# Opening of an FFT-mix and MoE kernel: x loaded in 96 rows, stage A stored with r outermost and in an order of its own, ten buffers for it, weights begun within stage A

## The chip, the cores and the metric

The kernel runs on one core of one Trainium2 chip, as one program. The metric is the device time of an execution in microseconds (us); it is compared by the median of several runs. A core has TensorE (PE in the profile; its weight loads are PEld), VectorE (DVE), ScalarE (ACT), GpSimd (POOL) and SyncE (SP). In this kernel every DMA is issued from SP, which handles its instructions in order, and the bytes are moved by the core's 16 DMA engines.

## What is computed

x has 8 images of 3008 rows and 256 columns. Each is transformed along its rows, mixed with a complex 256x256 matrix, biased, soft-thresholded and transformed back; the 24064 resulting rows then go through two matrix products with a squared ReLU between them.

```python
X = np.fft.rfft(x, axis=1)
Yr = Xr @ w_r - Xi @ w_i + b_r
Yi = Xr @ w_i + Xi @ w_r + b_i
Yr = np.sign(Yr) * np.maximum(np.abs(Yr) - lam, 0.0)      # lam = 0.01, the same for Yi
y = np.fft.irfft(Yr + 1j * Yi, n=3008, axis=1)
h = np.maximum(y.reshape(-1, 256) @ w_in, 0.0)            # w_in 256 x 2048
out = h * h @ w_out                                       # w_out 2048 x 256
```

x is float32; the two MoE weights are float64.

## The kernel before, in words

3008 is 47 x 64, so the transform is done in two stages of small matrix products: stage A transforms over the 47 (index n1), for 24 values of r, and stage B over the 64 (index n2). Between the two the data turns round through scratch memory in DRAM: `scr1[b]` holds [24 r][64 n2][512], where the 512 are the real and imaginary part (c) times 256 columns (d). `load_b` reads it back as rows (n, c) for two values of r, a "pair"; 12 pairs make an image. Stage B is `points_b` (matmuls with the table `tB`, line 237), then the mix with the weights (`psm`), the threshold, a turn (`zh`), and the way back over the 64 (`psc`, line 522), whose result goes to a second scratch `scr2[b]` (`store_c`, line 225). Stage D reads this (`load_d`, tile `din`), transforms back over the 47 (`psd`, line 275) and splits the result into a high and a low part, `xt`, on which the MoE works.

After the opening, one long planned sequence of 416 rounds runs the MoE: `mm1` (tile `ph`) and `mm2` (tile `po`), three matmuls for each product on high and low parts, and in between, at places named in a plan, the stages A, B and D of later images. The first round needs `xt` of the first chunk, the weights `wi_` and, two rounds later, `wo_`.

The opening is the function `start` (lines 290 to 592). Its instructions are issued in the order in which they are written, each engine in its own order. It prepares image 0 fully, image 1 up to the end of its stage A, and all weights and tables.

- **Loads.** `loads` issues the table `tU`, image 0 of x in two tiles `x0` (seven transfers), the mixing weights `raw`, and the biases. x lies in memory as 94 rows: row 2*n1 + w holds 32 blocks of 256 numbers. The 94 rows become 94 partitions.
- **Stage A of image 0** (`stage_a(0)`, lines 460 to 473 and 544 to 550): 16 steps. Each multiplies 94 rows of x by `tU` into 96 rows (line 467; order of the 96: w, part, r), copies the result from PSUM to an `ev` buffer on ACT (even steps) or DVE (odd steps), and stores the two halves of 256 columns with two DMAs (line 472) whose destination has the four (n, c) rows outermost and the 24 r inside. There are three `ev` buffers. In step 9 the mixing weights are split (`tables_start`); in steps 11 and 13 `weights()` is called.
- **`weights()`** (line 446) advances every weight block under way by one step and begins the next. There are 16 blocks of 512 KB: eight of `w_in`, eight of `w_out`. The steps of a block: load; nothing; absolute value on ACT; four instructions on DVE that put together a float32 from the two words of a float64; then for `w_in` a copy on ACT and a subtraction on POOL, for `w_out` two copies on ACT and four operations on POOL, a step later the copy into `wo` on ACT, a step later the subtraction on POOL. The load buffers (`w64`) are four, of which `raw` holds two at first.
- **The pair loop** (lines 558 to 580), n = 0 to 14: iteration n issues the load of pair n + 3 (tile `bin`, four buffers) and two loads of image 1 (`x1`, in tiles that later hold `wo`), then the threshold of pair n - 2, stage B of pair n, the mix of pair n - 1, the way back and the store of pair n - 3 (tile `evc`, from the same three `ev` buffers), one step of stage A of image 1 (from n = 2), the turn of pair n - 2, and `weights()`. At n = 10 `late` issues the loads of further tables, at n = 13 it works on them.
- **The tail** (lines 581 to 592): the inverse of the first chunk (`inverse`, two loads `din`, each followed by its matmuls, copies and split), mixed with the last steps of stage A of image 1 and of `weights()`.

A DMA store or load that writes or reads a buffer holds it until it has landed; a copy that wants the buffer waits for that on its engine, and what is queued behind it on that engine waits too.

Of the kernel before, what the change touches and what calls it, by code (L numbers as in the profile page):

```python
# [34 lines left out]
P = 128  # L35
S = 3008
N1 = 47
N2 = 64
NR = 24
NPAIR = NR // 2  # L40
D = 256
# [3 lines left out]
W = 5  # L45
GROUPS = [(g, min(W, N2 - g)) for g in range(0, N2, W)]


def _f32(bits):
    return float(np.array([bits], np.uint32).view(np.float32)[0])  # L50
# [30 lines left out]
def plain_rows():  # L81

    n2 = np.arange(N2).reshape(-1, 2)
    return ((64 * np.arange(N1)[:, None, None] + 47 * n2.T[None]) % S).reshape(2 * N1, N2 // 2)


def _cs(num, den):

    num = np.asarray(num) % den
    ang = 2.0 * np.pi * num / den  # L90
    c, s = np.cos(ang), np.sin(ang)
    c = np.where((4 * num) % (2 * den) == den, 0.0, c)
    s = np.where((2 * num) % den == 0, 0.0, s)
    return c, s


def tables():

    r = np.arange(NR)
    c47, s47 = _cs(np.outer(r, r), N1)  # L100
    wt = np.full(NR, 2.0 / S)
    wt[0] = 1.0 / S
    ta = np.zeros((120, 4, 120))
    td = np.zeros((120, 4, 120))
    for k, w in enumerate((W, N2 % W)):
        eye = np.eye(w)
        n = NR * w
        for part, m in enumerate((c47, -s47)):
# [24 lines left out]
    sgn = np.ones((P, 2, NR), np.float32)  # L133
    sgn[64:, 0] = sig.T
    sgn[:64, 1] = sig.T
    sgn[64:, 1] = sig.T

    n1 = np.arange(N1)
    tu = np.zeros((N1, 2, 2, 2, NR))
    for part, m in enumerate(_cs(np.outer(n1, r), N1)):  # L140
        for w in range(2):
            tu[:, w, w, part] = -m if part else m
    tu = tu.reshape(2 * N1, 4 * NR)
    return dict(t_u=tu.astype(np.float32), t_a=ta.astype(np.float32), t_b=tb.astype(np.float32), t_m=tm.astype(np.float32),
                t_d=td.astype(np.float32), sgn=sgn)


# [10 lines left out]

@with_exitstack
def fft_mix_moe(ctx: ExitStack, tc: tile.TileContext, xp, xu, w_r, w_i, b_r, b_i,  # L160
                w_in, w_out, t_u, t_a, t_b, t_m, t_d, sgn, outT):
    nc = tc.nc
    B = xp.shape[0] + xu.shape[0]
    NPLAIN = xu.shape[0]
# [16 lines left out]
    tB = ctile("tB", [P, NR + 1, N2])  # L181
# [22 lines left out]
    scr1, scr2 = {}, {}  # L204
# [50 lines left out]
    chunks = [flat[i:i + 2] for i in range(0, len(flat), 2)]  # L255
# [34 lines left out]
    def start():  # L290

        with ExitStack() as own:
# [4 lines left out]
            def tl(tag, shape=(P, 512), dt=F32, bufs=1, name=None):  # L297
                return sb.tile(list(shape), dt, tag=tag, name=name or tag, bufs=bufs)
# [2 lines left out]
                return pp.tile([P, 512], F32, tag="f", name=name)  # L301

            tM = tl("tM", (P, P))
            tU = tl("tU", (2 * N1, 4 * NR))
            row = tl("t", name="row")[:1]
            rows = [tl(f"row{k}", (1, 2 * D), F32R) for k in range(2)]
            ones = tl("z", name="ones")[:1, :P]
            one = tMs[:1, 0, :]
            nq = N2 // 4

            x0 = [const.tile([P, nq, D], F32, tag=f"wi{k}", name=f"x0{k}") for k in range(2)]
            x1 = []

            def load_x0(k, parts):
                for g0, g1 in parts:
                    nc.sync.dma_start(out=x0[k][:2 * N1, g0:g1, :], in_=xu[0, :, nq * k + g0:nq * k + g1, :])

            def load_x1():
                i = len(x1)
                if i < nq:  # L320
                    x1.append(const.tile([P, 2, D], F32, tag=f"wo{i % 2}{i // 2}", name=f"x1{i}"))
                    nc.sync.dma_start(out=x1[i][:2 * N1], in_=xu[1, :, 2 * i:2 * i + 2, :])


            raw = [tl("w64", (P, 512, 2), bufs=4, name="raw").rearrange("p n w -> p (n w)")[:, :3 * D]
# [15 lines left out]

            def more_loads():
                dma = nc.sync.dma_start
                dma(out=tB[:, 5:], in_=t_b[:, 5:])
                dma(out=sg, in_=sgn)
                dma(out=tM, in_=t_m)

# [98 lines left out]
            def weights(begin=True):  # L446

                for p in list(going):
                    if next(p, going) is going:
                        going.remove(p)  # L450
                p = next(pending, None) if begin else None
                if p is not None:
                    next(p)
                    going.append(p)
                return bool(going)
# [4 lines left out]
            def stage_a(b):  # L460

                scratch1(b)
                v = scr1[b].rearrange("r n (c d) -> (n c) r d", c=2)
                for i in range(nq):
                    t = x1[i][:2 * N1] if b else x0[i // 8][:2 * N1, 2 * (i % 8):2 * (i % 8) + 2, :]
                    o = pst("psa")[:4 * NR]
                    nc.tensor.matmul(o, tU, t.rearrange("p k d -> p (k d)"), start=True, stop=True)
                    e = tl("ev", bufs=3, name="eva")[:4 * NR]
                    copy(i, e, o)
                    for k in range(2):  # L470
                        q = 8 * i + 4 * k
                        nc.sync.dma_start(out=v[q:q + 4], in_=e[:, k * D:k * D + D])
                    yield

            xs, pm, zs, pc, got = {}, {}, {}, {}, {}
# [51 lines left out]
                store_c(0, i, ev)  # L527

            def inverse(c, xt):
                for u in range(len(chunks[c])):  # L530
                    t = tl("xl", bufs=2, name="din")
                    load_d(c, u, t)
                    yield
                    ps = points_d(c, u, t, pst("psd"))
                    v = tl("t", name="dv")[:, :2 * NR * W].rearrange("p (k m) -> p k m", k=2)
                    xf = tl("z", name="dx")[:, :2 * N1 * W].rearrange("p (k m) -> p k m", k=2)
                    m, (hi, lo) = part_x(c, u, xt)
                    nc.scalar.copy(v[:, :, :ps.shape[3]], ps[:, :, 1])
                    unfold(c, u, ps, v, xf)
                    split(xf[:, :, :m], hi, lo)  # L540

            loads()
            a0, a1 = stage_a(0), stage_a(1)
            for i, _ in enumerate(a0):
                if i == 3:
                    nc.sync.dma_start(out=tB[:, :5], in_=t_b[:, :5])
                if i == 9:
                    tables_start()
                if i in (11, 13):
                    weights()  # L550
            for i in range(3):
                load_pair(i)
# [5 lines left out]
            for n in range(NPAIR + 3):  # L558
                load_pair(n + 3)
                load_x1()  # L560
                load_x1()
                if 0 <= n - 2 < NPAIR:
                    pair_z(n - 2)
                if n < NPAIR:
                    pair_b(n)
                if 0 <= n - 1 < NPAIR:
                    pair_mix(n - 1)
                if n >= 3:
                    pair_c(n - 3)
                    pair_out(n - 3)  # L570
                if n >= 2:
                    next(a1)
                if 0 <= n - 2 < NPAIR:
                    pair_turn(n - 2)
                if n == NPAIR - 2:
                    nc.sync.dma_start(out=tD, in_=t_d)
                    next(late)
                if n == NPAIR + 1:
                    next(late, None)
                weights()  # L580
            inv = inverse(0, xt)
            next(inv)
            next(a1, None)
            weights()
            for _ in inv:
                next(a1, None)
                weights()
            for _ in a1:
                weights()
            while weights():  # L590
                pass
            return xt
# [278 lines left out]
    with tc.manual_schedule():  # L871
        for r in range(last + LAG):
            c, j = divmod(r, NU)
            run(r, "load")
            k = r - 1
            if k in hid:
                m, _ = halves(cols[k // NU])
# [15 lines left out]
            k = r - LAG  # L893
# [10 lines left out]
    assert not plan, sorted(plan)  # L904


_INS = ["xp", "xu", "w_r", "w_i", "b_r", "b_i", "moe_w_in", "moe_w_out", "t_u", "t_a", "t_b", "t_m", "t_d", "sgn"]


# [32 lines left out]
```

## Time and profile before

| | us |
|---|---|
| median of 3 runs | 2825.17 (2823.32 to 2825.36) |
| the profiled execution | 2825.74 |
| its span, first to last instruction | 2823.9 |
| PE busy in the span | 2652.5 (94%) |
| DVE busy | 2145.0 (76%) |
| ACT busy | 2031.8 (72%) |
| POOL busy | 52.6 (2%), all before 285 us |
| first `psb` matmul (stage B of pair 0) starts | 103.76 |
| last `psc` matmul (way back of pair 11) starts | 236.83 |
| first `ph` matmul (MoE) starts | 268.18 |

How to read the rows below. In the slices, the span is cut in 40 and each digit is the busy share in tenths. A row of windows has the stretch, its length, the busy time of each engine with the number of instructions, the clock that TensorE was granted (1 is full speed), the busy share of the 16 DMA engines, and what they moved in GB/s. A row of the timeline has the start, the time, engine, line, operation, output and inputs, their shapes, how many instructions are merged, and in brackets the idle time of that engine just before and what ended it. A row of waits has who waited for whom, the total, the number of waits and the longest. `SPq` rows are DMA issues; their sizes are those of one transfer.

### The profile page before, as it was taken

To read this page: it belongs to the slowest core of one execution; us is meant where nothing else is said; L and a number is where in the kernel's file an instruction comes from. 1 tells how busy PE (TensorE), PEld (TensorE's weight loads), DVE (VectorE), ACT (ScalarE), POOL (GpSimd) and SP (SyncE) were. 2 spreads that over 40 slices of the span, in tenths; PEclk is the share of its full clock that TensorE was granted. 3 is DMA by queue.
4 is the path that set the end of the run, shared out by engine and by line. 5 is a ranking of instruction groups with operands and counts; after the bars stand their busy time and mean duration, and the time that the engine had idled before them with its cause. 6 is when DMAs were issued, how large, how long until landed. Compare 5 with 4: busy or idle time off the path is not lost.

```text
span 2823.9 us, 45012 instructions
## 1 busy us (share of the span) xinstructions
PE 2652.5 (94%) x17816; PEld 2434.8 (86%) x17816; DVE 2145.0 (76%) x3301; ACT 2031.8 (72%) x2885; POOL 52.6 (2%) x60
## 2 busy tenths in 40 slices
PE   3556999999999999999999999999999999999998
PEld 0333999899998999999998999999999999999998
DVE  0336788878887888878888888888888888777776
ACT  0234787778777778777887787877878787766665
POOL 0015000000000000000000000000000000000000
PEclk9967999999999999999999999999999999999999
DMA  1443111221113111221113111221113111000000
GB/s 61 137 135 109 40 41 51 80 69 44 48 51 95 43 59 38 79 81 43 51 40 105 50 46 46 71 86 43 51 44 98 54 44 51 30 24 23 23 25 18
DMA packets 130756, 164.37 MB, mean 58 GB/s; under 512 B 10766, under 2 KB 94464, under 8 KB 130358
## 3 DMA queue, kind: packets, MB, share of 16 engines
q1 hardware_dynamic: 130546, 161.49, 18.9%
q8 instruction: 142, 2.33, 0.3%
q14 instruction: 68, 0.56, 0.1%
HBM read 86.47 MB, written 74.97 MB: 57 GB/s over the span
## 4 chain that ended last, share of the span: by engine, by line
PE 44%; DVE 23%; ACT 18%; issue 5%; DMA 1%; ACTq 0%; DVEq 0%; SPq 0%
ACT gh L879 9%; DVE gl L887 6%; PE ph L200 6%; PE ph L201 6%; PE ph L202 6%; PE po L202 6%; PE po L201 6%; PE po L200 5%; DVE g L836 4%; ACT g L830 3%; ACT g L829 3%; DVE g L837 3%; DVE g L838 2%; PE psm L202 2%; PE psb L237 2%
## 5 line engine op out<-in xcount | busy, mean ns | idle before, releaser
L887 DVE TENSOR_TENSOR gl<-g,gh 128x1652 fp32r<-128x1652 f32 (+1 forms) x416 | 770.2, 1851 | 346.0 <-ACT gh L879 346.0
L879 ACT CAST gh<-g 128x1652 fp32r<-128x1652 f32 (+1 forms) x416 | 645.8, 1552 | 401.8 <-DVE g L838 319.5
L200 PE MATMUL po<-gh,wo 128*128 128x236 f32 (+1 forms) x2912 | 810.0, 278 | 5.1 <-DVE o L861 1.7
L201 PE MATMUL po<-gl,wo 128*128 128x236 f32 (+1 forms) x2912 | 800.0, 275 | 2.4 <-DVE gl L887 2.4
L202 PE MATMUL po<-gh,wo 128*128 128x236 f32 (+1 forms) x2912 | 800.6, 275 | 0.0
L200 PE MATMUL ph<-xt,wi 128*128 128x470 f32 (+1 forms) x1664 | 634.8, 381 | 11.9 <-ACT g L829 8.1
L201 PE MATMUL ph<-xt,wi 128*128 128x470 f32 (+1 forms) x1664 | 624.1, 375 | 4.0 <-DVE xt L783 3.9
L202 PE MATMUL ph<-xt,wi 128*128 128x470 f32 (+1 forms) x1664 | 619.0, 372 | 0.0
L200 PEld LDWEIGHTS po<-gh,wo 128*128 128x128 f32 x2912 | 556.1, 191 | 19.0 <-DVE o L861 5.9
L201 PEld LDWEIGHTS po<-gl,wo 128*128 128x128 f32 x2912 | 555.5, 191 | 8.9 <-DVE gl L887 2.8
L202 PEld LDWEIGHTS po<-gh,wo 128*128 128x128 f32 x2912 | 557.2, 191 | 0.0
L829 ACT ACTIVATE g<-ph 128x472 f32<-128x472 f32 (+1 forms) x832 | 417.6, 555 | 68.9 <-PE ph L202 68.8
L830 ACT ACTIVATE g<-g 128x944 f32<-128x944 f32 (+1 forms) x416 | 408.8, 983 | 13.2
L200 PEld LDWEIGHTS ph<-xt,wi 128*128 128x128 f32 x1664 | 315.6, 190 | 49.0 <-ACT g L829 12.6
L202 PEld LDWEIGHTS ph<-xt,wi 128*128 128x128 f32 x1664 | 314.3, 189 | 39.5
L201 PEld LDWEIGHTS ph<-xt,wi 128*128 128x128 f32 x1664 | 316.7, 190 | 34.5 <-DVE xt L783 6.9
L836 DVE TENSOR_TENSOR g<-g 128x472 f32<-128x472 f32 (+1 forms) x416 | 266.1, 640 | 38.4 <-ACT g L830 26.7
L838 DVE TENSOR_TENSOR g<-g 128x236 f32<-128x236 f32 (+1 forms) x416 | 166.5, 400 | 14.4
L837 DVE TENSOR_TENSOR g<-g 128x236 f32<-128x236 f32 (+1 forms) x416 | 166.5, 400 | 14.2
L202 PE MATMUL psm<-wm,xl 128*128 128x256 f32 (+1 forms) x552 | 162.1, 294 | 3.6 <-DVE xl L692 3.6
L200 PE MATMUL psm<-wm,xh 128*128 128x256 f32 (+1 forms) x552 | 161.4, 292 | 0.0
L201 PE MATMUL psm<-wm,xh 128*128 128x256 f32 (+1 forms) x552 | 159.6, 289 | 0.0
(107 smaller groups left out, 2804.4 us busy)
## 6 DMA issues: line engine op xcount, KB each, us to landing
bin<-s SPq DMA_DIRECT2D x96, 256.0 KB
s<-evc SPq DMA_DIRECT2D x96, 256.0 KB
din<-s SPq DMA_DIRECT2D x96, 240.0 KB
xin<-in_xp_dram SPq DMA_DIRECT2D x72, 240.0 KB
s<-eva SPq DMA_DIRECT2D x72, 240.0 KB
outT_dram<-o SPq DMA_DIRECT2D x96, 118.0 KB
outT_dram<-o SPq DMA_DIRECT2D x96, 117.0 KB
s<-eva SPq DMA_DIRECT2D x64, 96.0 KB
```

The source lines that it names most:

```text
L200: nc.tensor.matmul(out, l0, r0, start=start, stop=False, **kw)
L201: nc.tensor.matmul(out, l0, r1, start=False, stop=False, **kw)
L202: nc.tensor.matmul(out, l1, r0, start=False, stop=stop, **kw)
L237: nc.tensor.matmul(ps[:, k, :, q, :], tv[:, q, k], tB[:, 0:r + 2:r + 1], start=True, stop=True)
L829: nc.scalar.activation(g[:, t:4:2, :m], ph[:, :, t * t0:t * t0 + m], AF.Relu)
L830: nc.scalar.activation(g[:, 0:4, :m], g[:, 0:4, :m], AF.Square)
L836: nc.vector.tensor_sub(g[:, 4:6, :m], g[:, 1:4:2, :m], g[:, 0:2, :m])
L837: nc.vector.tensor_sub(g[:, 6, :m], g[:, 3, :m], g[:, 4, :m])
L838: nc.vector.tensor_sub(g[:, 1, :m], g[:, 6, :m], g[:, 2, :m])
L879: nc.scalar.copy(gg[k][0][:, :, :m], hid[k][:, :, :m])
L887: nc.vector.tensor_sub(gg[k][1][:, :, :m], hid.pop(k)[:, :, :m], gg[k][0][:, :, :m].bitcast(F32))
```

## The change

It is all in the opening and in its tables.

- x of images 0 and 1 is laid out in 96 rows: the last two repeat the first two, and `tU` has zeros for them. The tiles are loaded and multiplied with 96 partitions.
- The columns of `tU` are reordered, so that stage A's 96 result rows stand in the order r, w, part.
- Image 1's stage A stores have r outermost in memory and the four (n, c) rows inside; where each number ends up is unchanged.
- Image 0's stage A result is stored with one DMA a step, all 512 columns of a row in one piece. The rows of `scr1[0]` then stand in another order than those of `scr1[1]`. A reordered table `t_b0` makes up for it while image 0 is worked on; after that the whole of `tB` is loaded again from `t_b`.
- Image 0's stage A results use buffers of three tags in turn, four of `bin`, three of `ev`, three of `ld`: ten.
- `weights()` is called in steps 9, 11, 13 and 15 of stage A, and in the pair loop only up to n = 12.
- `late` issues its loads at n = 7 in place of 10.
- The step of stage A of image 1 at n = 14 is left out of the loop. After the loop both `din` loads are issued, then the load of `tB`, then the four steps of stage A that remain, with `weights()` after the second and the fourth, then the inverse, then the rest of `weights()`.

```diff
+NU1 = 96
...
     rows = ((64 * np.arange(N1)[:, None, None] + 47 * n2.T[None]) % S).reshape(2 * N1, N2 // 2)
+    return np.concatenate([rows, rows[:NU1 - 2 * N1]])
...
-    tu = np.zeros((N1, 2, 2, 2, NR))
+    tu = np.zeros((NU1 // 2, 2, NR, 2, 2))
     for part, m in enumerate(_cs(np.outer(n1, r), N1)):
         for w in range(2):
-            tu[:, w, w, part] = -m if part else m
-    tu = tu.reshape(2 * N1, 4 * NR)
+            tu[:N1, w, :, w, part] = -m if part else m
+    tu = tu.reshape(NU1, 4 * NR)
+
+    tb0 = tb.reshape(N2 // 4, 2, 2, 2, NR + 1, N2).transpose(0, 2, 3, 1, 4, 5).reshape(P, NR + 1, N2)
...
-                    nc.sync.dma_start(out=x0[k][:2 * N1, g0:g1, :], in_=xu[0, :, nq * k + g0:nq * k + g1, :])
+                    nc.sync.dma_start(out=x0[k][:NU1, g0:g1, :], in_=xu[0, :, nq * k + g0:nq * k + g1, :])
...
-                    nc.sync.dma_start(out=x1[i][:2 * N1], in_=xu[1, :, 2 * i:2 * i + 2, :])
+                    nc.sync.dma_start(out=x1[i][:NU1], in_=xu[1, :, 2 * i:2 * i + 2, :])
...
-                dma(out=tB[:, 5:], in_=t_b[:, 5:])
+                dma(out=tB[:, 5:], in_=t_b0[:, 5:])
...
-                v = scr1[b].rearrange("r n (c d) -> (n c) r d", c=2)
+                v = scr1[b].rearrange("r n (c d) -> r (n c) d", c=2)
...
-                    e = tl("ev", bufs=3, name="eva")[:4 * NR]
+                    tag, n = ("ev", 3) if b else (("bin", 4), ("ev", 3), ("bin", 4), ("ld", 3))[i % 4]
+                    e = tl(tag, bufs=n, name="eva")[:4 * NR]
                     copy(i, e, o)
-                    for k in range(2):
+                    if b == 0:
+                        v0 = scr1[b].rearrange("r n e -> r (n e)")[:, 4 * i * 2 * D:4 * (i + 1) * 2 * D]
+                        nc.sync.dma_start(out=v0.rearrange("r (m e) -> r m e", m=4), in_=e)
+                    for k in range(2 * b):
                         q = 8 * i + 4 * k
-                        nc.sync.dma_start(out=v[q:q + 4], in_=e[:, k * D:k * D + D])
+                        nc.sync.dma_start(out=v[:, q:q + 4], in_=e[:, k * D:k * D + D])
...
-                for u in range(len(chunks[c])):
-                    t = tl("xl", bufs=2, name="din")
+                got = [tl("xl", bufs=2, name="din") for _ in chunks[c]]
+                for u, t in enumerate(got):
                     load_d(c, u, t)
-                    yield
+                yield
+                for u, t in enumerate(got):
                     ps = points_d(c, u, t, pst("psd"))
...
                 if i == 3:
-                    nc.sync.dma_start(out=tB[:, :5], in_=t_b[:, :5])
+                    nc.sync.dma_start(out=tB[:, :5], in_=t_b0[:, :5])
                 if i == 9:
                     tables_start()
-                if i in (11, 13):
+                if i in (9,11,13,15):
                     weights()
...
-                if n >= 2:
+                if 2 <= n < NPAIR + 2:
                     next(a1)
...
-                if n == NPAIR - 2:
+                if n == NPAIR - 5:
                     nc.sync.dma_start(out=tD, in_=t_d)
                     next(late)
                 if n == NPAIR + 1:
                     next(late, None)
-                weights()
+                if n < NPAIR + 1:
+                    weights()
             inv = inverse(0, xt)
             next(inv)
-            next(a1, None)
-            weights()
+            nc.sync.dma_start(out=tB, in_=t_b)
+            for i, _ in enumerate(a1):
+                if i % 2 == 1:
+                    weights()
             for _ in inv:
-                next(a1, None)
-                weights()
-            for _ in a1:
-                weights()
+                pass
             while weights():
                 pass
```

More of the change, by code (lines that the diff above doesn't have):

```diff
@@ L83, in plain_rows @@
     n2 = np.arange(N2).reshape(-1, 2)
-    return ((64 * np.arange(N1)[:, None, None] + 47 * n2.T[None]) % S).reshape(2 * N1, N2 // 2)
+    rows = ((64 * np.arange(N1)[:, None, None] + 47 * n2.T[None]) % S).reshape(2 * N1, N2 // 2)
+    return np.concatenate([rows, rows[:NU1 - 2 * N1]])
 def _cs(num, den):
@@ L138, in tables @@
     n1 = np.arange(N1)
-    tu = np.zeros((N1, 2, 2, 2, NR))
+    tu = np.zeros((NU1 // 2, 2, NR, 2, 2))
     for part, m in enumerate(_cs(np.outer(n1, r), N1)):
         for w in range(2):
-            tu[:, w, w, part] = -m if part else m
-    tu = tu.reshape(2 * N1, 4 * NR)
-    return dict(t_u=tu.astype(np.float32), t_a=ta.astype(np.float32), t_b=tb.astype(np.float32), t_m=tm.astype(np.float32),
+            tu[:N1, w, :, w, part] = -m if part else m
+    tu = tu.reshape(NU1, 4 * NR)
+    tb0 = tb.reshape(N2 // 4, 2, 2, 2, NR + 1, N2).transpose(0, 2, 3, 1, 4, 5).reshape(P, NR + 1, N2)
+    return dict(t_u=tu.astype(np.float32), t_a=ta.astype(np.float32), t_b=tb.astype(np.float32), t_b0=tb0.astype(np.float32), t_m=tm.astype(np.float32),
                 t_d=td.astype(np.float32), sgn=sgn)
@@ L160, in fft_mix_moe @@
 def fft_mix_moe(ctx: ExitStack, tc: tile.TileContext, xp, xu, w_r, w_i, b_r, b_i,
-                w_in, w_out, t_u, t_a, t_b, t_m, t_d, sgn, outT):
+                w_in, w_out, t_u, t_a, t_b, t_b0, t_m, t_d, sgn, outT):
     nc = tc.nc
@@ L303, in start @@
             tM = tl("tM", (P, P))
-            tU = tl("tU", (2 * N1, 4 * NR))
+            tU = tl("tU", (NU1, 4 * NR))
             row = tl("t", name="row")[:1]
@@ L462, in stage_a @@
                 scratch1(b)
-                v = scr1[b].rearrange("r n (c d) -> (n c) r d", c=2)
+                v = scr1[b].rearrange("r n (c d) -> r (n c) d", c=2)
                 for i in range(nq):
-                    t = x1[i][:2 * N1] if b else x0[i // 8][:2 * N1, 2 * (i % 8):2 * (i % 8) + 2, :]
+                    t = x1[i][:NU1] if b else x0[i // 8][:NU1, 2 * (i % 8):2 * (i % 8) + 2, :]
                     o = pst("psa")[:4 * NR]
                     nc.tensor.matmul(o, tU, t.rearrange("p k d -> p (k d)"), start=True, stop=True)
-                    e = tl("ev", bufs=3, name="eva")[:4 * NR]
+                    tag, n = ("ev", 3) if b else (("bin", 4), ("ev", 3), ("bin", 4), ("ld", 3))[i % 4]
+                    e = tl(tag, bufs=n, name="eva")[:4 * NR]
                     copy(i, e, o)
-                    for k in range(2):
+                    if b == 0:
+                        v0 = scr1[b].rearrange("r n e -> r (n e)")[:, 4 * i * 2 * D:4 * (i + 1) * 2 * D]
+                        nc.sync.dma_start(out=v0.rearrange("r (m e) -> r m e", m=4), in_=e)
+                    for k in range(2 * b):
                         q = 8 * i + 4 * k
-                        nc.sync.dma_start(out=v[q:q + 4], in_=e[:, k * D:k * D + D])
+                        nc.sync.dma_start(out=v[:, q:q + 4], in_=e[:, k * D:k * D + D])
                     yield
@@ L904, in fft_mix_moe @@
     assert not plan, sorted(plan)
-_INS = ["xp", "xu", "w_r", "w_i", "b_r", "b_i", "moe_w_in", "moe_w_out", "t_u", "t_a", "t_b", "t_m", "t_d", "sgn"]
+_INS = ["xp", "xu", "w_r", "w_i", "b_r", "b_i", "moe_w_in", "moe_w_out", "t_u", "t_a", "t_b", "t_b0", "t_m", "t_d", "sgn"]
 def kernel(**inputs):
```

## The prediction

> **What bounds the kernel now.** I read the page first: its slices, to see where TensorE is not full.
>
> ```profile
> span 2823.9 us, 45012 instructions
> ...
> PE   3556999999999999999999999999999999999998
> ...
> DMA  1443111221113111221113111221113111000000
> ```
>
> A slice is 70.6 us. Only the first four are short of TensorE work; from the fifth on PE is full. The profiled execution took 2825.74 us, 1.84 more than its span, and the median of the runs shown is 2825.17, 0.57 below it. Next come the stretches of the opening (columns: stretch, length, busy PE, PEld, DVE, ACT, POOL, granted clock, DMA share of 16 engines, GB/s).
>
> ```profile
> 0.00:103.70 103.70, 30.60 (x32) 7.17 (x32) 8.03 (x13) 9.70 (x16) 0.20 (x4) 1.00 0.23 82
> 103.70:131.00 27.30, 27.24 (x108) 19.81 (x109) 16.33 (x27) 11.22 (x20) 3.94 (x3) 1.00 0.48 157
> 131.00:241.00 110.00, 70.11 (x210) 40.92 (x209) 49.74 (x89) 40.32 (x78) 21.62 (x27) 0.75 0.46 146
> 241.00:268.20 27.20, 8.57 (x23) 4.34 (x21) 16.73 (x18) 12.10 (x24) 25.63 (x27) 0.56 0.16 50
> 268.20:284.00 15.80, 12.26 (x42) 10.02 (x43) 5.34 (x8) 7.45 (x9) 1.18 (x1) 0.76 0.20 62
> 284.00:2640.00 2356.00, 2330.29 (x16269) 2193.05 (x16268) 1920.85 (x2966) 1832.37 (x2594) 0.00 (x0) 1.00 0.19 55
> ```
>
> After 284 us TensorE is busy 2330 of 2356 us, and the change touches nothing there. So the question is how much earlier the first `ph` matmul (268.18 us) can start. Up to 241 us no engine is full, and the DMA engines seem idle by half. Fine windows (length, PE, clock, DMA share, GB/s) show otherwise:
>
> ```profile
> 2.00:4.00 2.00, 0.00 (x0) 1.00 0.11 30
> ...
> 36.00:38.00 2.00, 2.00 (x3) 1.00 0.13 53
> ...
> 82.00:84.00 2.00, 0.00 (x0) 1.00 0.27 96
> ...
> 106.00:108.00 2.00, 2.00 (x9) 1.00 1.03 373
> ...
> 140.00:142.00 2.00, 0.00 (x0) 0.50 0.13 51
> ```
> ```profile
> 254.00:254.50 0.50, 0.00 (x0) 0.50 0.68 258
> ```
>
> While only x loads of 94 rows run, the share stands at 0.13, which is 2 of 16 engines (0.125), each at some 25 GB/s. While only stage A stores run, whose outermost dimension counts 4, it is 0.27, 4 of 16, at 24 GB/s each. Loads of 128 rows fill all sixteen. The `din` load, with 24 outermost in memory and 120 partitions, reaches 0.68, 11 engines. The engines used thus go with what divides the outermost counts: 2 for 94, 4 for 4, 12 for 24 with 120, 16 for 128. And what is queued behind those few engines waits (columns: total us, times, longest):
>
> ```profile
> DVE eva L458 <- DMA s<-eva: 71.4, 6, 52.6
> ACT eva L458 <- DMA s<-evc: 60.4, 4, 20.2
> ```
>
> A store spread over 16 engines (`s<-evc`) lands only when its share on the two loaded engines has, so the copies that need its `ev` buffer stand, and TensorE behind them.
>
> **The change, part by part.** Sizes of the transfers (KB each):
>
> ```profile
> bin<-s SPq DMA_DIRECT2D x96, 256.0 KB
> s<-evc SPq DMA_DIRECT2D x96, 256.0 KB
> ...
> s<-eva SPq DMA_DIRECT2D x64, 96.0 KB
> w<-in_moe_w_in_dram SPq DMA_DIRECT2D x8, 512.0 KB
> ...
> x<-in_xu_dram SPq DMA_DIRECT2D x18, 188.0 KB
> ```
>
> (1) *Loads of x in 96 rows.* No row shows 96. Bounds: 2 engines, as 94 has, and 16, as 128 has. By the divisors above 96 goes to 16, and I take that. The Trainium skill ("DMA: Bandwidth & Descriptors", section "Why a DMA increments its semaphore by 16 and not by 1") states this as a rule: the largest count up to 16 that divides the outermost dimension of both sides; the rows 0.13, 0.27 and 0.68 agree. By it the sum stays as it stands here; by the 94-row row alone it would be the third rival's.
>
> (2) *Stage A stores with r outermost.* 24 in memory against 96 partitions: 12 divides both. Bounds: 4 engines as now, and the 11 to 12 of `din`; I take 12. For image 0 they also become 16 stores of 192 KB in place of 32, in an order of their own that `t_b0` answers; that halves SP's issues there.
>
> (3) *Stage A of image 0 now.* x loads: 16 x 192 KB over 16 engines is 192 KB an engine; `raw` 32 KB, the first part of `tB` 10 KB, stores 16 x 192 KB over 12 engines 256 KB, the three weight loads that are issued ahead of the last store 96 KB: 586 KB, or 600 kB, on each of the busiest twelve. An engine moved 24 GB/s at 82 us and 22.6 at 106 (373/16/1.03); 20 at worst:
>
> ```profile
> 220.00:240.00 20.00, 14.75 (x34) 6.52 (x33) 16.30 (x25) 12.99 (x26) 9.75 (x13) 0.78 0.66 210
> ```
>
> (210/0.66/16.) At 22 GB/s it is 27.3 us, with 25 and 30 as ends. TensorE beside it needs, at its slow pace, 3.73 us for two steps, 30 us for sixteen, and at the fast one 1.02 a step:
>
> ```profile
> 34.56 3.73 PE L467 MATMUL psa<-x,tU 94*96 94x512 f32 x4 [3.60 <-DMA x<-in_xu_dram]
> ...
> 123.75 1.02 PE L467 MATMUL psa<-x,tU 94*96 94x512 f32 x2
> ```
>
> It starts at about 4 us (the first bytes move in the window from 2 us) and speeds up on the way, as it does after 104 us; so it is ahead of the transfers, unless it stays slow (34 us, then +5). Ten buffers let copies run ahead of landings; three would stall here. The x bytes follow those of `tU`, near 2.8 us by that window, so the last store lands at about 30.5. Then comes the load of the first pair:
>
> ```profile
> 100.78 1.42 SPq L217 DMA_DIRECT2D bin<-s  x3
> ```
> ```profile
> 103.76 3.75 PE L237 MATMUL psb<-tB,bin 128*128 128x128 f32 x16 [25.03 <-issue]
> ...
> 124.61 1.05 PE L237 MATMUL psb<-tB,bin 128*128 128x128 f32 x8
> ...
> 130.86 1.07 PE L237 MATMUL psb<-tB,bin 128*128 128x128 f32 x8
> ...
> 153.62 2.08 PE L522 MATMUL psc<-zh,tM 128*128 128x512 f32 x2 [18.06 <-ACT zh L518]
> ...
> 216.01 1.05 PE L237 MATMUL psb<-tB,bin 128*128 128x128 f32 x8
> ...
> 231.68 2.07 PE L522 MATMUL psc<-zh,tM 128*128 128x512 f32 x2 [3.88 <-ACT zh L518]
> ...
> 236.83 2.05 PE L522 MATMUL psc<-zh,tM 128*128 128x512 f32 x2 [1.37 <-ACT wmf L368]
> ...
> 268.18 0.73 PE L200 MATMUL ph<-xt,wi 128*128 128x470 f32 x1 [3.72 <-DVE eva L458]
> ```
>
> 3 us from issue to the first `psb`, plus half a us for the receipt: first `psb` at **34** in place of 103.76: **69.8 us** gained. The wait added: at step 13 ACT takes the first weight block's absolute value, and its copy of step 14 is queued behind; that load lands at some 22 us, when the stores still have a backlog, so it costs nothing; without that cover up to 3 us.
>
> (4) *The pair loop, pairs 0 to 5.* 27.1 us (103.76 to 130.86) with TensorE never idle, its slow first 8 us included. Kept.
>
> (5) *Pairs 5 to 11.* Now 85.15 us (130.86 to 216.01), 14.2 a pair. The load on engines 0 and 1 says why: per iteration two x loads of 94 KB, 48 KB of stage A stores, 32 of weights, 16 each of `bin` and `evc`: 300 KB, 12.3 us at 25 GB/s. After: 24 + 16 + 32 + 16 + 16 = 104 KB, 4.8 us at 22. TensorE's own iteration is 6.25 (124.61 to 130.86), and becomes the bound: 6 x 6.25 = 37.5, **47.6 us** gained. Three `ev` buffers serve two copies an iteration, a us apart, so the store of `evc` has some 6.6 us to land before its buffer is wanted; with weights, `bin` and x loads issued right after the preceding stores their 72 KB are gone in 3.4 us, so it finds its rings empty. The loads that `late` issues (1.2 MB, 76 KB an engine, 3.5 us) now come at pair 7, when ring time is 4.8 + 3.5 against 6.25: up to 2 us of backlog, which the buffer's margin hides. DVE and ACT had 16.3 and 13.0 us of work in the 20 from 220 us, with POOL running, which is 5.1 and 4.1 a pair.
>
> (6) *Pair 11's `psb` to its `psc`.* Now 20.8 us, of which 3.88 is a wait for `zh`, behind an ACT copy that stood for an `evc` store. Without it 16.5: **4.3 us**.
>
> (7) *The tail.* Now 31.35 us from the last `psc` to the first `ph`.
>
> ```profile
> 246.15 0.45 POOL L195 TENSOR_TENSOR tMs<-tM,tMs 128x128 fp32r<-128x128 f32 x1
> 246.56 2.06 POOL L438 TENSOR_TENSOR wo<-w,wo 128x896 fp32r<-128x896 f32 x1
> ...
> 264.44 0.45 POOL L432 TENSOR_TENSOR w<-w,w 128x128 f32<-128x128 f32 x1
> ```
> ```profile
> 264.52 0.58 ACT L194 CAST xt<-dx 128x470 fp32r<-128x470 f32 x1 [0.91 <-DVE dx L283]
> ```
> ```profile
> 265.13 2.30 DVE L195 TENSOR_TENSOR xt<-dx,xt 128x470 fp32r<-128x470 f32 x1 [0.65 <-ACT xt L194]
> ```
>
> POOL ends the tables 9.8 us after the last `psc` and then works off `w_out`, four rounds of about 4 us before the `xt` split; ACT waits for its buffers in between. Two of those rounds come from the calls of `weights` at n = 13 and 14; with weights begun two calls earlier these are gone and two rounds are left: 8 us, so ACT reaches the inverse at +16.5 to +17.8. By then both `din` loads, issued together once the last `evc` has landed, are in. The inverse is two chains of copy, two DVE sums, ACT split and DVE split, 2.4 to 3.6 us each by whether POOL is active: first `ph` at +22.5. **8.9 us** gained; ends +20.5 and +31.35. The four stage A steps of image 1 that are left, moved ahead of the inverse, fit below POOL's time. The new load of the whole `tB` (800 KB, 2.6 us at 318 GB/s) is issued behind `din` and ahead of these stores; its reader, the first `psb` of image 1, came 18 us after the first `ph`. It costs nothing; without that cover 2.6 us.
>
> Sum: 69.8 + 47.6 + 4.3 + 8.9 = 130.6. First `ph` at 137.6, the execution 2825.74 - 130.6 = 2695.1, against a median of runs 0.57 lower, say **2695**.
>
> **The rivals.** *All sixteen rings become the bound.* The loop needs 1.6 MB an iteration; at 250 GB/s of mixed reads and writes it takes 6.6 us, with queueing some 8.5 over nine iterations (+20), and stage A +6: 2721. For it: no row shows such a mix for long; against it, 373 GB/s at 106 us and the ends above. [...]
>
> *The loop keeps its pace*, because the `evc` stores are late for another reason: 133.1 us from first `psb` to last `psc` stay, 34 + 133.1 + 22.5 = 189.6: 2747. Against it: pairs 2 to 5 run at 6.25.
>
> *The change does not do what it says: 96 rows stay on two engines.* x ends at 67 us as now, first `psb` at 76; rings 0 and 1 carry 272 KB an iteration, 11.6 us: ten us less loop: 76 + 123 + 22.5 = 221: 2779.
>
> *Slower: stores with r outermost go down one engine.* 3.1 MB at 24 GB/s take 131 us, first `psb` at 144, 40 later; the loop gains 5 and the tail 9: 2852. It decides below about 1.25 engines; at two the change is faster again. Against it: `din` at 0.68 with the same 24.
>
> **How the numbers follow.** Forecast 0.66 (nearly all of it within 2682 to 2712), rings 0.20, pace kept 0.08, two engines 0.04, slower 0.02. The range 2682 to 2728 takes in the forecast and most of the rings' case. A difference under 0.2% counts as none. Faster 0.97, same 0.01, slower 0.02.
>
> **What would show it.** DMA share near 1.0 within the first 10 us; no wait of `eva` on `s<-eva` over 5 us; first `psb` near 34, pairs 6.25 us apart with clock 1.00; hardly any `eva` wait on `s<-evc`; last `psc` near 115, first `ph` near 138, and the rest unchanged. Wrong it is if a window of stage A or of the loop keeps a share of 0.13 or 0.27, or if pairs come over 8 us apart.

## The result, and the profile after

The changed kernel takes 2703.75 us (median of 4 runs, 2700.33 to 2704.11); the kernel before, in 4 runs, 2825.03 (2823.32 to 2825.36). The ratio is 0.9569, interval 0.9553 to 0.9586: 121 us gained where 130 were forecast. The profiled execution took 2704.11. Its page, the lines that answer to those of before:

```profile
span 2702.3 us, 44970 instructions
...
PE   7889999999999999999999999999999999999998
...
DMA  8611113111221112211132112311123121000000
```

A slice is 67.6 us now. Three are short of TensorE work where four were, and they read 7, 8 and 8 where there were 3, 5, 5 and 6. The DMA engines are busy at the very start. The same stretches as before, cut at the same events (first `psb`, `psb` of pair 5, `psb` of pair 11, last `psc`, first `ph`; columns as in the table of before):

```profile
0.00:39.00 39.00, 19.11 (x32) 6.23 (x33) 13.37 (x21) 11.27 (x19) 1.66 (x5) 0.85 0.86 248
39.00:66.50 27.50, 27.48 (x107) 20.04 (x108) 18.91 (x30) 12.41 (x22) 5.21 (x4) 0.84 0.90 258
66.50:104.30 37.80, 37.77 (x158) 25.28 (x157) 27.98 (x52) 24.67 (x47) 14.15 (x17) 1.00 0.84 250
104.30:125.20 20.90, 15.79 (x49) 8.16 (x48) 19.77 (x31) 15.34 (x30) 10.24 (x15) 0.87 0.38 124
125.20:147.50 22.30, 9.14 (x26) 4.33 (x27) 12.26 (x13) 8.66 (x19) 17.96 (x18) 0.73 0.39 116
163.00:2518.00 2355.00, 2329.28 (x16260) 2192.25 (x16259) 1920.02 (x2964) 1832.79 (x2595) 0.00 (x0) 1.00 0.19 55
```

Up to 104 us the DMA engines are 0.84 to 0.90 busy, where they stood at 0.23 to 0.48; between 39 and 104 us TensorE is never idle; the plan's long part is as it was. What is left below full TensorE work are the first 39 us and the 43 between pair 11 and the first `ph`. The events in TensorE's timeline:

```profile
4.14 12.03 PE L472 MATMUL psa<-x,tU 96*96 96x512 f32 x16 [4.14 <-DMA x<-in_xu_dram]
...
39.02 3.75 PE L242 MATMUL psb<-tB,bin 128*128 128x128 f32 x16 [15.35 <-DMA bin<-s]
...
66.48 1.05 PE L242 MATMUL psb<-tB,bin 128*128 128x128 f32 x8
...
104.26 1.05 PE L242 MATMUL psb<-tB,bin 128*128 128x128 f32 x8
...
120.11 2.05 PE L531 MATMUL psc<-zh,tM 128*128 128x512 f32 x2 [3.26 <-DVE zh L526]
...
125.23 2.04 PE L531 MATMUL psc<-zh,tM 128*128 128x512 f32 x2 [1.37 <-ACT wmf L373]
...
147.50 0.76 PE L205 MATMUL ph<-xt,wi 128*128 128x470 f32 x1 [10.52 <-ACT xt L199]
...
162.05 1.05 PE L280 MATMUL psd<-tD,din 120*128 120x120 f32 x8
```

The last row is the first `psd` of the next chunk, from where TensorE is full to the end; that took 2540.2 us, and 2540.5 before. Against the prediction, stretch by stretch:

| stretch | before | predicted | after | after less predicted |
|---|---|---|---|---|
| start to first `psb` | 103.76 | 34 | 39.02 | +5.0 |
| pairs 0 to 5 | 27.10 | 27.1 | 27.46 | +0.4 |
| pairs 5 to 11 | 85.15 | 37.5 | 37.78 | +0.3 |
| pair 11's `psb` to last `psc` | 20.82 | 16.5 | 20.97 | +4.5 |
| last `psc` to first `ph` | 31.35 | 22.5 | 22.27 | -0.2 |
| first `ph` | 268.18 | 137.6 | 147.50 | +9.9 |

The waits of the opening (total, times, longest) hold the two misses, and the absence of the old ones: where the longest `eva` waits were 52.6 and 20.2 us, they are 3.8 and 2.7 now.

```profile
PE psb L242 <- DMA bin<-s: 15.3, 1, 15.3
...
ACT w L385 <- DMA w<-in_moe_w_in_dram: 8.1, 3, 5.4
...
ACT eva L463 <- DMA s<-eva: 3.8, 1, 3.8
...
PE psc L531 <- DVE zh L526: 3.3, 1, 3.3
...
DVE eva L463 <- DMA s<-evc: 2.7, 1, 2.7
```

### The profile page after: what moved, and what is told of

Same layout as the page of the kernel before. It is cut to its first block, busy times and chain, and to the rows that moved or that the text cites. A ratio compares the mean times of both kernels' runs of the same rounds, so it can differ in the third digit from the quotient of the medians.

```text
span 2702.3 us, 44970 instructions
## 1 busy us (share of the span) xinstructions
PE 2624.7 (97%) x17816; PEld 2425.5 (90%) x17816; DVE 2147.3 (79%) x3301; ACT 2031.8 (75%) x2885; POOL 51.3 (2%) x60
## 3 DMA queue, kind: packets, MB, share of 16 engines
q1 hardware_dynamic: 129858, 162.44, 20.2%
## 4 chain that ended last, share of the span: by engine, by line
PE 47%; DVE 26%; ACT 19%; issue 5%; DMA 2%; POOL 1%; SPq 0%; ACTq 0%; DVEq 0%; POOLq 0%
ACT gh L889 10%; DVE gl L897 7%; PE ph L205 6%; PE ph L206 6%; PE ph L207 6%; PE po L207 6%; PE po L206 6%; PE po L205 6%; DVE g L846 4%; ACT g L840 3%; ACT g L839 3%; DVE g L847 3%; DVE g L848 2%; PE psm L207 2%; PE psb L242 2%
## 5 line engine op out<-in xcount | busy, mean ns | idle before, releaser
L205 PE MATMUL ph<-xt,wi 128*128 128x470 f32 (+1 forms) x1664 | 634.9, 382 | 16.9 <-ACT xt L199 10.5
L205 PEld LDWEIGHTS ph<-xt,wi 128*128 128x128 f32 x1664 | 315.7, 190 | 52.6 <-ACT xt L199 10.7
```

Of the source, the lines that this page charges most:

```text
L205: nc.tensor.matmul(out, l0, r0, start=start, stop=False, **kw)
```

## The experiments

Twelve kernels, each the changed kernel with one change, the last with three. A `...` in a diff stands for lines left out. Ratios are to the kernel before; positions are those of one profiled execution each.

### What each part of the change is worth

**Loads of x in 94 rows again.**

```diff
-NU1 = 96
+NU1 = 94
```

> x in 94 rows again, all else as in the changed kernel. Theory (a load runs on as many DMA engines as divide its outermost count, so 94 rows get two): DMA share near 0.13 while only x loads run, first psb at 70 to 76 us, pairs about 11.6 us apart as long as x of image 1 is loaded, total 2765 to 2790. Rival (the stores' order brought the gain, the loads did not matter): first psb within 5 us of 39 and total under 2715.

Measured: 2796.34 us (2795.18 to 2797.51), ratio 0.9896 (0.9876 to 0.9916). First `psb` 86.11, pairs 5 to 11 82.4 us (115.11 to 197.50), 13.7 a pair. 92.6 of the 121 us are gone with this one number. Total and pace, too, lie outside what was expected (2765 to 2790, 11.6 a pair). TensorE's windows (length, busy, clock, DMA share, GB/s) and the waits of this kernel:

```profile
6.00:16.00 10.00, 4.01 (x4) 1.00 0.17 61
```
```profile
ACT eva L463 <- DMA s<-evc: 36.1, 2, 19.2
ACT eva L463 <- DMA s<-eva: 29.0, 1, 29.0
```

The share falls to 0.17 beside 1.07 with 96 rows, and the old kind of wait is back in the loop. That the loads' rows carry the loop's gain is thereby shown; the rival that they don't matter falls. First `psb` came 10 us later than the top of what I expected. Within stage A a copy now waits 29.0 us for a store; that the store was late for its share on the two loaded engines is argued. SP, too, issued the first store only at 42.07.

**Image 1's stores as before** (four rows outermost; its own table `tU1` keeps the place of each number).

```diff
...
-                v = scr1[b].rearrange("r n (c d) -> r (n c) d", c=2)
+                v = scr1[b].rearrange("r n (c d) -> (n c) r d", c=2)
...
-                        nc.sync.dma_start(out=v[:, q:q + 4], in_=e[:, k * D:k * D + D])
+                        nc.sync.dma_start(out=v[q:q + 4], in_=e[:, k * D:k * D + D])
```

> Only image 1's stage A stores go back to the four (n, c) rows outermost (with a table of their own for the old order of the 96 rows). Theory: four engines then carry 24 + 48 + 32 + 16 + 16 = 136 KB an iteration, 6.3 us at 22 GB/s, just the 6.25 of TensorE: pairs 6.3 to 7 us apart, total 2704 to 2714. Rival (this order carries much of the loop's gain): pairs over 9 us apart, total above 2725.

Measured: 2702.44 (2698.34 to 2704.20), ratio 0.9562 (0.9547 to 0.9576); pairs 5 to 11 in 38.0 us, 6.3 a pair, the low end of what was expected, and the total just below it. No difference to the changed kernel that can be told: once x is off the two engines, 48 KB an iteration on four engines are hidden.

**Both images' stores as before**, two a step for image 0 too, without `t_b0`.

```diff
...
-                    if b == 0:
-                        v0 = scr1[b].rearrange("r n e -> r (n e)")[:, 4 * i * 2 * D:4 * (i + 1) * 2 * D]
-                        nc.sync.dma_start(out=v0.rearrange("r (m e) -> r m e", m=4), in_=e)
-                    for k in range(2 * b):
+                    for k in range(2):
...
-                        nc.sync.dma_start(out=v[:, q:q + 4], in_=e[:, k * D:k * D + D])
+                        nc.sync.dma_start(out=v[q:q + 4], in_=e[:, k * D:k * D + D])
```

> The stage A stores of both images go back to two a step with four rows outermost, and t_b is used throughout; loads in 96 rows, ten buffers and the calls of weights stay. Theory: in stage A of image 0 four engines carry about 1100 KB, 46 to 50 us, so the first psb comes at 53 to 58 us in place of 39, and the total is 2718 to 2735. Rival (stage A is set by the loads of x and ACT's waits): first psb below 44, total below 2710.

Measured: 2722.10 (2720.44 to 2723.75), ratio 0.9633 (0.9614 to 0.9653); first `psb` 57.48, then the loop as fast as with the change. A window of its stage A:

```profile
20.00:30.00 10.00, 6.57 (x12) 0.84 0.31 109
```

The share, 0.31, is that of 5 of 16 engines while the stores work off. So the form of the stores and their halved number together are worth 18 us, all of it in stage A of image 0, within both bounds of what was expected. The two were not tried apart.

**Three buffers instead of ten.**

```diff
-                    tag, n = ("ev", 3) if b else (("bin", 4), ("ev", 3), ("bin", 4), ("ld", 3))[i % 4]
+                    tag, n = "ev", 3
```

> Stage A of image 0 uses the three ev buffers alone, as before. Theory (with full rings a store takes 5 to 8 us to land, so three buffers pass one step every 2 to 2.7 us): first psb at 44 to 50 in place of 39, total 2708 to 2716. Rival (the bytes on the rings bind anyway): first psb at 39 to 41, total 2703 to 2706.

Measured: 2707.26 (2707.22 to 2707.29), ratio 0.9584 (0.9564 to 0.9603); first `psb` 44.81. The ten buffers are worth 5.8 us at the first `psb` and 3.5 of the total; in the profiled execution the rest went in pairs 0 to 5, which took 25.11 us here and 27.46 in the changed kernel (see the end).

### Why the first `psb` came at 39 and not at 34

In the changed kernel the engines are full and still slow:

```profile
6.00:16.00 10.00, 10.00 (x15) 1.00 1.07 244
```

244 GB/s over 16 engines at a share of 1.07 are 14 GB/s an engine; I had taken 22. Three kernels ask what slows them: 128 rows (the table zero beyond 94), 112 rows, and 96 rows with one more block of 1 KB in each row of x, so that the rows lie 33 KB apart in memory instead of 32.

```diff
-NU1 = 96
+NU1 = 128
```

> x of images 0 and 1 in 128 rows, the last 34 repeating the first (a third more bytes); tU has zeros for them. In the changed kernel the DMA engines moved only 220 to 270 GB/s at full share from 6 to 16 us. Theory S (96 partitions load the SBUF side unevenly): with all 128 the rate from 6 to 16 us rises above 310 GB/s and the first psb stays within 1 us of 39. Theory M (the memory side limits, by the 32 KiB from row to row): the rate stays at 230 to 270, x arrives 4 us later, first psb at 42 to 44, total 2706 to 2712.

```profile
6.00:16.00 10.00, 8.38 (x19) 1.00 0.99 374
```

```diff
+    xu = np.concatenate([xu, xu[:, :, :1]], 2)
```

> x of images 0 and 1 is laid out in memory with 33 blocks of 1 KiB a row, the last one never read, so that rows lie 33 KiB apart in place of 32; nothing else. Theory M (the memory side limits, by the power of two): the rate from 6 to 16 us rises above 300 GB/s and the first psb comes at 35 to 37.5, total 2700 to 2703. Theory S (the SBUF side limits): rate 220 to 270 as before, first psb within 1 us of 39, total 2702 to 2705.

```profile
6.00:16.00 10.00, 8.17 (x15) 1.00 1.04 249
```

```diff
-NU1 = 96
+NU1 = 112
```

> x in 112 rows, between 96 (244 GB/s from 6 to 16 us) and 128 (374 GB/s). Theory G (the rate goes gradually with the rows, 64 of which use one half of the ways into SBUF): 280 to 320 GB/s. Theory E (only shares of eight rows an engine are fast): 235 to 265 GB/s.

```profile
6.00:16.00 10.00, 9.02 (x15) 1.00 1.06 249
```

Totals: 2700.34 (2700.07 to 2700.60) with 128 rows, ratio 0.9559 (0.9540 to 0.9578); 2703.51 (2701.35 to 2706.42) with the other pitch, ratio 0.9569 (0.9553 to 0.9585); 2706.64 with 112 (one run). The distance of the rows is not it: 244 GB/s at 32 KB and 249 at 33. The rate does not grow step by step with the rows either: 96 and 112 give 244 to 249, 128 gives 374, which is 23.6 GB/s an engine at a share of 0.99, a little more than the prediction had assumed. In these kernels an engine was fast with eight rows of a load and slow with six or seven. But the first `psb` comes only 2.0 us sooner (37.01; both theories had it at 38 or later): 128 rows move a third more bytes of x, and the chain of that kernel still runs through the first weight block, issued at 21.97 and waited for 5.7 us.

The rest of the miss is waits that I had priced at nothing. The chain of waits and ACT's timeline of the changed kernel:

```profile
3.52 7.95 DMA raw<-in_w_r_dram
...
11.56 8.10 DMA s<-eva
...
24.04 5.50 DMA w<-in_moe_w_in_dram
...
31.56 4.32 DMA s<-eva
35.95 2.94 DMA bin<-s
```
```profile
19.74 0.58 ACT L463 COPY eva<-psa 96x512 f32<-96x512 f32 x1 [3.80 <-DMA s<-eva]
...
29.56 0.66 ACT L385 ACTIVATE w<-w 128x512 f32<-128x512 f32 x1 [5.40 <-DMA w<-in_moe_w_in_dram]
30.12 0.57 ACT L463 COPY eva<-psa 96x512 f32<-96x512 f32 x1
```

The chain starts with the stores. The first one was ready at 6.75, when its copy ended, but SP issued it at 11.56, just after the first `raw` load had landed; what held SP no view shows. That store took 8.10 us to land, and the copy of step 8, the fifth to use one of the four `bin` buffers, stood 3.80 us for it. The first weight block is issued at 24.04, behind further stores, and lands at 29.54; ACT stands 5.40 us for it, and the copy of step 14 behind it waits as well. SP issues the stores of steps 14 and 15 one after the other from 30.71, and the last lands at 35.9. Putting `weights()` back to where it was in stage A takes the 5.40 away, and with it two of the four weight loads issued there:

```diff
-                if i in (9,11,13,15):
+                if i in (11, 13):
```

> weights() is called in steps 11 and 13 of stage A, as before, in place of 9, 11, 13 and 15. Theory (the first weight block's landing, for which ACT waits with the copy of step 14 behind it, and the weight blocks ahead of the last stores set the end of stage A): no ACT wait for w within stage A, first psb at 34 to 36 in place of 39; the tail after the last psc grows by 6 to 9, total 2705 to 2711. Rival (the end of stage A is set by x and the stores alone): first psb at 38 to 39.5, total 2710 to 2714.

Measured: 2706.75 (2704.58 to 2708.40), ratio 0.9581 (0.9565 to 0.9597). First `psb` 36.50, 2.5 us sooner, half a us outside what was expected: that is the price of the two earlier calls, the wait and the added loads together. What they buy is seen only behind the first `ph`. That comes at 141.65, 5.9 us sooner than in the changed kernel (2.7 of it are pairs 0 to 5, see the end); yet the next chunk's `psd` starts at 162.33, no sooner than 162.05. POOL's, ACT's and TensorE's timelines of this kernel say why:

```profile
148.27 4.11 POOL L443 TENSOR_TENSOR wo<-w,wo 128x896 fp32r<-128x896 f32 x2
```
```profile
152.41 1.02 ACT L839 ACTIVATE g<-ph 128x472 f32<-128x472 f32 x2 [3.13 <-POOL wo L443]
```
```profile
153.48 0.76 PE L205 MATMUL ph<-xt,wi 128*128 128x470 f32 x1 [7.23 <-ACT g L839]
...
162.33 1.05 PE L280 MATMUL psd<-tD,din 120*128 120x120 f32 x8
```

The weight blocks left over end on POOL at 152.4. The first square `g`, which reads `ph`, starts on ACT only then, after a wait of 3.13 us for POOL's `wo`, and TensorE waits 7.23 us for it after its first twelve `ph` matmuls. I had expected the delay ahead of the first `ph` (6 to 9 us); it was 1.4 there and the rest behind. Begun earlier, the weights cost 2.5 us in stage A and give back more at the end: the median is 3.0 us higher without the earlier calls, though the intervals overlap.

### Why pair 11's way back gained nothing

The prediction had 4.3 us from here, as the wait for an `evc` store would go. In its place stands this, in the chain, on DVE and on POOL:

```profile
91.75 8.11 DMA s<-evc
99.96 0.69 DVE eva L463
```
```profile
111.19 0.68 DVE L518 SCALAR_TENSOR_TENSOR z<-psm,t 128x512 f32<-128x512 f32 x1
...
114.19 2.21 DVE L388 TENSOR_SCALAR w<-w 128x512 uint32<-128x512 uint32 x1
...
117.78 0.68 DVE L518 SCALAR_TENSOR_TENSOR z<-psm,t 128x512 f32<-128x512 f32 x1
...
120.86 0.43 DVE L388 TENSOR_SCALAR w<-w 128x512 uint32<-128x512 uint32 x1
```
```profile
113.98 2.14 POOL L443 TENSOR_TENSOR wo<-w,wo 128x896 fp32r<-128x896 f32 x1 [0.73 <-ACT wo L441]
```

Two suspects: the `evc` store of 91.75, which took 8.11 us to land behind the loads of `late`; or DVE's own pace, 6.59 us from `z` to `z` where TensorE's iteration is 6.25. Line 388 takes 0.43 us alone (at 120.86) and 2.21 beside POOL's 2.14 on `wo`, and ends 0.3 us after that (116.40 against 116.12). The first suspect is tested by `late` at n = 10 again:

```diff
-                if n == NPAIR - 5:
+                if n == NPAIR - 2:
```

> late issues its table loads at n = 10, as before, in place of n = 7. Theory (these loads delayed the evc store of pair 7 to 8 us, DVE stood 2.7 us for it and, with 6.6 us of work an iteration, never caught up, so TensorE waited for zh at the end): no DVE wait on s<-evc over 1 us, last psc 2.5 to 4.5 us earlier, total 2699 to 2702. Rival (DVE's work beside a busy POOL sets the end in any case): the wait is gone, the last psc comes within 1 us of 125.2, total 2703 to 2705.

Measured: 2705.16 (2698.82 to 2706.43), ratio 0.9572 (0.9557 to 0.9586). DVE's wait at 99.96 is gone, and `psb` to `psc` takes 20.4 us, 0.6 less. The last `psc` came 3.1 us sooner, as was expected if the store were the cause, but 2.3 of that are pairs 0 to 5, and the median is no lower. The waits moved: now an ACT copy stands for an `evc` store, and TensorE for ACT's `zh` behind it, as in the kernel before.

```profile
ACT eva L463 <- DMA s<-evc: 3.9, 1, 3.9
```
```profile
117.43 1.58 PE L531 MATMUL psc<-zh,tM 128*128 128x512 f32 x2 [3.99 <-ACT zh L527]
```

So this run puts one late store in the place of another and does not settle the matter. The kernel with `weights()` back in steps 11 and 13 says more. There DVE stood 3.33 us for an `evc` store, longer than the 2.66 of the changed kernel, and yet the stretch took only 19.22 us (98.76 to 117.98), with DVE's copies in place:

```profile
117.98 2.05 PE L531 MATMUL psc<-zh,tM 128*128 128x512 f32 x2 [1.67 <-DVE zh L526]
```

POOL had done two `wo` subtractions by then (at 101.68 and 107.36), where the changed kernel has four (94.40 to 113.98). So the late store alone does not make the stretch long, and DVE's work beside POOL's is the likelier cause. The second suspect is tested by giving DVE's PSUM copies of n = 8 to 13 to ACT:

```diff
...
-                (nc.vector.tensor_copy if n % 2 else nc.scalar.copy)(out, in_)
+                on_act = 8 <= turn[0] < NPAIR + 2 or n % 2 == 0
+                (nc.scalar.copy if on_act else nc.vector.tensor_copy)(out, in_)
...
```

> From the changed kernel: in the iterations n = 8 to 13 all copies of stage A and evc results go to ACT, none to DVE. Theory (DVE's 6.5 us an iteration in the last pairs, with instructions stretched to 2.2 us beside POOL, make zh late): DVE has 0.6 us less an iteration, and psb of pair 11 to the last psc takes 17 to 18.5 us in place of 21, total 2699 to 2702. Rival (ACT becomes the late engine, or the stores' landing does): 20 to 21 us, total 2702 to 2706.

Measured: 2700.05 (2698.91 to 2700.91), ratio 0.9555 (0.9540 to 0.9569). The stretch is 19.17 us, 1.8 shorter, between the two expectations, and TensorE's waits in it are now on ACT:

```profile
115.59 1.10 PE L534 MATMUL psc<-zh,tM 128*128 128x512 f32 x2 [2.49 <-ACT zh L530]
...
120.16 2.08 PE L534 MATMUL psc<-zh,tM 128*128 128x512 f32 x2 [1.99 <-ACT zh L530]
```

So DVE's load is a part of it, and what is taken off DVE is soon short on ACT. The total says less: the profiled span is 4.5 us shorter (2697.8), of which 2.6 are pairs 0 to 5 (24.83 us). The third try takes tables off this stretch and off the tail: the loads and splits of `late` are spread over n = 2 to 9, two splits (`wm`, `tM`) go behind the inverse, `weights()` runs at every n, and the rest of stage A of image 1 stands ahead of the inverse.

```diff
...
-                if n == NPAIR - 5:
-                    nc.sync.dma_start(out=tD, in_=t_d)
+                if 2 <= n < 10:
                     next(late)
-                if n == NPAIR + 1:
-                    next(late, None)
-                if n < NPAIR + 1:
-                    weights()
+                weights()
...
```

> From the changed kernel: the loads of late are spread over n = 2 to 9, the sums of the mix table and the split of tA are done in n = 5 to 7, the splits of the mix table and of tM after the inverse; in place of the tables, weights() is called at n = 13 and 14 and all of image 1's stage A ends ahead of the inverse. Theory (POOL's 10 us on tables stand ahead of the last weight blocks, and ACT waits with the inverse for those): from the last psc to the first ph 14 to 17 us in place of 22.3, total 2694 to 2700. Rival (the din loads and ACT's own work set the tail): 20 us or more, total 2702 to 2706.

Measured: 2703.47 (2698.98 to 2704.99), ratio 0.9562 (0.9546 to 0.9578). Last `psc` to first `ph` fell to 18.4 us from 22.3, but `psb` to `psc` rose to 22.8 and the time stands. TensorE's longest wait in it is for DVE again:

```profile
128.31 2.04 PE L540 MATMUL psc<-zh,tM 128*128 128x512 f32 x2 [4.28 <-DVE zh L535]
```

### The three together

128 rows, the tables spread as above, and the copies of n = 8 to 14 on ACT:

```diff
-NU1 = 96
+NU1 = 128
...
+                on_act = turn[0] >= 8 or n % 2 == 0
+                (nc.scalar.copy if on_act else nc.vector.tensor_copy)(out, in_)
...
```

> Three changes of the runs before together: x in 128 rows, the tables' work spread as before, and all stage A and evc copies of n = 8 to 14 on ACT. Theory (DVE beside POOL is what takes back the gain of the spread tables): psb of pair 11 to the last psc takes 18 to 20 us in place of 22.8, the last psc to the first ph 16 to 18.5, the first psb comes at 37 to 38, total 2692 to 2698. Rival (the last pairs and the tail share one chain that only moves its waits about): first ph within 2 us of 143, total 2698 to 2703.

Measured: 2697.50 (5 runs, 2696.56 to 2701.55), ratio 0.9543 (0.9530 to 0.9557), the fastest here, 6 us below the changed kernel, whose interval it touches at 0.9553 to 0.9557; in the profiled execution 2.6 us of its lead are pairs 0 to 5. First `psb` 37.33, last `psc` to `ph` 17.35 as expected; `psb` to `psc` 21.3 and not 18 to 20:

```profile
115.62 2.05 PE L543 MATMUL psc<-zh,tM 128*128 128x512 f32 x2 [2.50 <-ACT zh L539]
...
121.68 1.35 PE L543 MATMUL psc<-zh,tM 128*128 128x512 f32 x2 [2.44 <-ACT zh L539]
```

## Why the prediction was right, and where its terms were off

*Parts (1) and (2), which engines a transfer uses.* Right. 96 rows fill all engines (a share of 1.07, against 0.17 with 94), and the new stores against the old are worth 18 us; no window shows these stores alone, so that they run on 12 engines is not shown. One thing I had not separated: for image 1 the form is worth nothing that can be told.

*Part (3), stage A.* Right in its mechanism (full engines from 6 us, no `eva` wait on `s<-eva` above 3.8), 5.0 us short in its size. The rate "at 22 GB/s" an engine came from rows with 128-row loads at full share; with 96 rows it was 14 while x loaded. "Ten buffers let copies run ahead of landings" held only to step 8, where ACT stood 3.80 us. And "so it costs nothing" of the first weight block was wrong, as was its landing "at some 22 us": the load was issued at 24.04. Without the two earlier calls of `weights` the first `psb` came 2.5 us sooner, within the 3 given for a failed cover; 128 rows bring 2.0. The two were not tried together, and both act on one chain, so that they add up to 4.5 of the 5.0 is not shown; in five kernels with the same stage A the first `psb` stood between 38.66 and 39.75. The "half a us for the receipt" has no row: the first `bin` load was issued 0.07 us after the last store had landed.

*Parts (4) and (5), the loop.* Right: 27.46 and 37.78 us against 27.1 and 37.5, pairs 6.25 us apart at clock 1.00. That part (4) came out so close is luck: in eight of the other kernels these pairs took 24.8 to 25.4 us. The rival of sixteen rings as the bound did not come: the share is 0.84 to 0.90 with TensorE never idle. Nor did the rival in which the loop keeps its old pace. The backlog of `late`, "which the buffer's margin hides", was not hidden on its engine (DVE stood 2.66 us at 99.96, for a store that took 8.11 where I gave 6.6), but issuing it later only moved the wait.

*Part (6).* Wrong: no gain where 4.3 us were forecast (and 20.8 less the wait of 3.88 is 16.9, not 16.5). The step that failed is "Without it 16.5": it took a named wait off the stretch as though nothing stood close behind. DVE did: busy 15.97 of the 20.80 us there before (216.0 to 236.8), it was busy 19.77 of 20.90 after (the window above). My rate for DVE, 5.1 us a pair, was the busy share of a window, 16.3 of 20 us, times 6.25. An iteration's work was 6.59 us: in each of the last three iterations a `wo` subtraction of POOL meets a DVE instruction and adds 1.2 to 1.8 us to it. The trace of before has this too, on an instruction that takes 0.69 us elsewhere:

```profile
224.61 2.50 DVE L385 SCALAR_TENSOR_TENSOR w<-w,w 128x512 uint32<-128x512 uint32 x1
```

The Trainium skill ("SBUF — State Buffer", section "Who interferes with whom") says that VectorE and GpSimd share a pair of ports, and that where a VectorE instruction uses this pair, whichever of the two is first holds it for its whole instruction and the other blocks. Line 388, which took 2.21 us in place of 0.43 and ended 0.3 us after POOL's instruction, agrees. How much of the 4.5 us is DVE's stays open: 1.8 came off with its copies, 1.8 also with fewer subtractions on POOL beside it, and no run brought the stretch below 19.09 (that with x in 94 rows).

*Part (7), the tail.* Right, 22.27 against 22.5, and ACT reached the inverse 16.8 us after the last `psc` (142.00), where 16.5 to 17.8 were forecast; the reload of `tB` brought no `psb` wait (the only one on a DMA is that for the first `bin`). But the first `ph` was too early a place to end the sum: with the weights back in steps 11 and 13 it came 5.9 us sooner and the time was no shorter.

*The sign and the slower rival.* The slower rival, stores on one engine, did not come: the new stores gained 18 us on the old.

## What to carry to other kernels

A mean DMA share of 0.13 or 0.27 can mean two or four engines full and everything behind them late; count the outermost dimension of both sides of each large transfer, and pad it (with zeros in the table that multiplies it) before looking for anything subtler. When a wait is taken away, add up every engine's work at the new pace, with what meets it at that pace, and price the wait on a load by when its issue comes, not by when its bytes could move. Measure an opening by where TensorE becomes full for good, not by its first matmul of the next stage.

## What the runs showed of the hardware that was not expected

All 16 engines at a share of 1.07 moved only 244 GB/s with loads of 96 rows, 249 with 112, and 374 at 0.99 with 128: a full share is no full rate. The Trainium skill ("SBUF — State Buffer", section "Door 1: The DMA port swizzle") maps partitions 0 to 63 onto eight of the buffer's 16 ports and 64 to 127 onto the other eight. By that map 112 rows load the ports more evenly than 96, yet the rate was the same; the ports have no row here, so the cause of the step between 112 and 128 stays open.

Between profiled executions, pairs 0 to 5 differ by some 2.5 us, and not by what the edits touch: they took 27.1 to 27.6 us in the changed kernel and in those with only 128 rows, only 112 rows or only the tables spread, and 24.8 to 25.4 in the eight others that load x in at least 96 rows. With `late` at n = 10, where they took 25.19, the other runs were up to 7.6 us slower than the profiled one. TensorE had idled ahead of its first `psb` and came back at half clock. The window from 44 to 49 us, first of the changed kernel, then of the one with `late` at n = 10:

```profile
44.00:49.00 5.00, 5.00 (x16) 0.60 1.05 304
```
```profile
44.00:49.00 5.00, 5.00 (x26) 1.00 1.06 305
```

By windows of 1 us the clock is back at 48 us in one and at 43 in the other; 5 us at half speed make the 2.5 us. Positions of single executions are therefore compared here by stretches, and totals by medians; differences of 2 to 3 us in either are not sure. Why the clock varies is open; and before the change, where the first 16 `psb` matmuls took 3.75 us as well, its row says 1.00.
